# A linear-attention and two-layer feed-forward kernel on one core: the first eight attention units reordered, four weight tiles loaded earlier

## The chip, the cores and the metric

One core of a Trainium2 chip runs the whole program. The metric is the device time in microseconds (us), as the median of several runs.

## The reference, cut to what matters

```python
for t in range(S):                                  # B=4, H=8, S=768, D=64
    state = gamma * state + k[:, :, t] (outer) v[:, :, t]
    y[:, :, t] = scale * q[:, :, t] @ state         # attention with decay
x = y as (3072 tokens, 512)
h = x @ w_in;  x = (h - tanh(h)) @ w_out            # 512 -> 2048 -> 512
h = x @ w_in2; solu = h * softmax(h)                # 512 -> 1024
out = layernorm(solu) * g_ln @ w_out2               # 1024 -> 512
```

The weights arrive as 64-bit floats; the kernel takes them as pairs of 32-bit words and builds single precision from them itself ("decoding").

## The kernel before, in words

The attention is cut into 24 units, numbered k = 4c + b: chunk c of 128 time steps (six) of batch b (four). The linear recurrence becomes, for a unit, a set of small TensorE products of 64x64: **scores** (q against k, and k against v, 64 recorded matmuls and as many weight loads) and **output** (q against the running state, and the masked scores against v: 48 matmuls in chunk 0, 64 in later chunks). Between them the scores are masked into `pr`, and the states `sb` and `sa` are updated.

A unit needs, in this order: two transfers of 512 KB (`z`, the halves with q and k and with k and v), and for each chunk a table `tab` of 256 KB; `prepare(k)` (line 235), which scales q by the table on POOL (L245) and v on ACT (L252, four heads) and POOL (L256, the rest); the scores on PE (L233), their mask (L327, DVE), `sb` (L333 on ACT in chunk 0, L335 on DVE later) and `sa` (L338, DVE); the output on PE (L233), which ACT copies to `xf` (L299, L302, L303) and DVE completes with an addition (L307); and `split_x` (line 340), which splits `xf` into a high and a low part: ACT casts the high part (L345), DVE or POOL subtracts for the low one (L346).

Units 0 to 3 make the first block of 512 tokens, units 4 to 7 the second. The program's first stage works off units 0 to 7, then PE goes on with the first feed-forward layer: `products_h(s, f)` (line 349, L357) multiplies token block s by weight tile f, 12 matmuls of 512 columns, `less_tanh` applies tanh (L364, ACT) and the subtraction (L365, DVE). In the text H(f, b) stands for tile f on block b. Units 8 to 15 are woven between the following H.

A weight tile goes through four steps of `Decoder.to` (line 175): step 0 loads it (`raw`, 512 KB, L125, SP's queue); step 1 is one ACT instruction (L131); step 2 is four DVE instructions (L138, L139, L142, L145); step 3 is a cast on ACT (L154) and a subtraction on DVE (L155), after which ACT's queue issues the store of the decoded tile (L189, `wfd`, 256 KB).

Who sets the order: a scheduler places instructions on each engine by a modelled timeline, except those that `pin` (line 100) keeps in the order of the program. PE's products of this stage are all pinned. In the first stage `prepare`, `unit` (with `amid`) and the decoding of tiles 0 to 2 are pinned on ACT, DVE and POOL too. Loads are not pinned; the transfers that SP issues leave in the order in which the scheduler put them, and an issue that must wait holds up all behind it. `tab` has two buffers, so the table of chunk 2 waits for the last use of the table of chunk 0 (the L245 of unit 3), that of chunk 3 for the L245 of unit 7.

PE's order in the first stage: scores 0, scores 1, output 0, scores 2, output 1, scores 3, ..., output 5, scores 7, output 6, H(0,0), output 7, H(1,0), then the main loop with H(0,1), H(1,1), H(2,0), H(2,1), H(3,0) and so on. In the loop of the first stage (line 655) each turn calls `unit(k, k + 2)`: output of unit k, its copies, `prepare(k + 3)`, the addition, `split_x(k)`, scores of unit k + 2 and their evacuation, in this order on each engine.

Of the kernel before, what the change touches and what calls it, by code (L numbers as in the profile page):

```python
# [29 lines left out]
AF = mybir.ActivationFunctionType  # L30
ALU = mybir.AluOpType
# [4 lines left out]
B, H, S, D = 4, 8, 768, 64  # L36
# [29 lines left out]
def col(p, h):  # L66

    return h ^ (p & 1)
# [21 lines left out]
def body(ctx: ExitStack, tc, z, w_in, w_out, w_in2, w_out2, g_ln, cst, tab, out):  # L90
    nc = tc.nc
# [8 lines left out]
    def pin(ins, on=True):  # L100

        if on:
            tc.keep_in_program_order(ins)

    def t4(shape, dtype, name):
        return big.tile(shape, dtype, tag="t4", name=name)
# [52 lines left out]
    late = [False]  # L159

    def fix(ins):
        pin(ins, late[0])
# [42 lines left out]
    zq, zv, tb, vs, qs, pt, sa, sb, xt = {}, {}, {}, {}, {}, {}, {}, {}, {}  # L205
    xf_of = {}
# [2 lines left out]

    def load_tab(c):  # L210
        tb[c] = stp.tile([P, NP * P], F32, tag="tab", name="tab", bufs=2)
        (nc.sync if c else nc.scalar).dma_start(out=tb[c], in_=tab[c])

    def load_half(k, half):
        t = t4([P, 2, NP, P], F32, "z")
        nc.sync.dma_start(out=t.rearrange("p a b c -> p (a b c)"), in_=z[2 * k + half])
        (zv if half else zq)[k] = t

    def load_units(upto):
        while loaded[0] < min(upto, NU):  # L220
            k = loaded[0]
            if k // B not in tb:
                load_tab(k // B)
            for half in range(2):
                load_half(k, half)
            loaded[0] += 1

    def rows(h):
        return slice(h * D, (h + 1) * D)

    def products(todo):
        for o, a, b in todo:
            pin(nc.tensor.matmul(o, a, b, start=True, stop=True, skip_group_check=True), held[0])  # L233
# [28 lines left out]
    def unit(ko, ks, hold=False, pool=ps_r, tag="r", opool=ps_r, engs=None, amid=None):  # L262

        if ko is not None:
            c, b = divmod(ko, B)
            q, v, po, st = qs.pop(ko), vs.pop(ko), pt.pop(ko), (sa.pop(ko, None), sb.pop(ko))
            w = [opool.tile([P, 2, 4 * D], F32, tag="r", name="out") for _ in range(2)]  # L270
            fr = [t[:, 0, :].rearrange("q (i t) -> q i t", i=2) for t in w]
            y = [t[:, 1, :].rearrange("q (h i t) -> q h i t", h=2, i=2) for t in w]

            steps = range(2) if c else (1,)
            products([
                (
                    fr[h][rows(col(2 * i + odd, h)), i, rows(ab)],
                    st[ab][rows(h), 2 * i + odd, :], q[rows(h), 2 * i + odd, rows(ab)],
                )
                for i in range(2) for ab in steps for odd in range(2) for h in range(2)  # L280
            ])
            products([
                (
                    y[ab][rows(col(p, h)), h, p // 2, :], v[rows(ab), 2 * p + h, :],
                    po[rows(ab), h, p, :],
                )
                for p in range(NP) for ab in range(2) for h in range(2)
            ])
            if hold:
                if b == 0:  # L290
                    xf_of[c] = xfp.tile([P, 2, 2, SB], F32, tag=f"xf{c % 2}", name="xf")
                xf = xf_of[c][:, :, :, b * P : (b + 1) * P]
            else:
                xf = t2([P, 2, 2, P], F32, "xf")
            xa = xf.rearrange("q h i t -> q (h i) t")
            ya = [t.rearrange("q h i t -> q (h i) t") for t in y]
            if c:
                for h in range(2):
                    pin(nc.scalar.copy(xf[:, h, :, :], fr[h]), amid or late[0])  # L299
            else:  # L300
                for h in range(2):
                    pin(nc.scalar.copy(xf[:, h, :, rows(1)], fr[h][:, :, rows(1)]), amid or late[0])  # L302
                pin(nc.scalar.copy(xa[:, :, rows(0)], ya[0]), amid or late[0])  # L303
            if amid:
                amid()
            for ab in steps:
                pin(nc.vector.tensor_tensor(  # L307
                    xa[:, :, rows(ab)], xa[:, :, rows(ab)], ya[ab], ALU.add
                ), amid or late[0])
            if not hold:  # L310
                split_x(c, b, xf, engs or (nc.gpsimd, nc.gpsimd), amid or late[0])
        if ks is not None:
            c = ks // B
            kt, kv, v, q = zq.pop(ks)[:, 1, :, :], zv.pop(ks), vs[ks], qs[ks]
            w = [pool.tile([P, 2, 4 * D], F32, tag=tag, name="sc") for _ in range(2)]
            sc, gn = ([t[:, n, :].rearrange("q (p t) -> q p t", p=NP) for t in w] for n in range(2))
            products([
                (sc[h][rows(ab), p, :], kt[rows(h), p, rows(ab)], q[rows(h), p, rows(ab)])
                for p in range(NP) for h in range(2) for ab in range(2)
            ])  # L320
            products([
                (gn[ab][rows(h), p, :], kv[rows(ab), 0, p, rows(h)], v[rows(ab), 2 * p + h, :])
                for p in range(NP) for ab in range(2) for h in range(2)
            ])
            pr = t2([P, 2, NP, D], F32, "pr")
            for h in range(2):
                pin(nc.vector.tensor_tensor(  # L327
                    pr[:, h, :, :], sc[h], mask.unsqueeze(1).to_broadcast([P, NP, D]), ALU.mult
                ), amid or late[0])
            pt[ks] = pr  # L330
            sb[ks] = stp.tile([P, NP, D], F32, tag="sb", name="sb", bufs=3)
            if c == 0:
                nc.scalar.copy(sb[ks], gn[0])  # L333
            else:
                fix(nc.vector.tensor_tensor(sb[ks], sa[ks], gn[0], ALU.add))  # L335
            if c < NC - 1:
                sa[ks + B] = stp.tile([P, NP, D], F32, tag="sa", name="sa")
                fix(nc.vector.tensor_tensor(sa[ks + B], sb[ks], gn[1], ALU.add))  # L338

    def split_x(c, b, xf, engs, fixed=False):  # L340
        if b == 0:
            xt[c] = [[t4([P, 2, SB], F32R, f"x{n}") for _ in range(2)] for n in "hl"]
        for h in range(2):
            xh, xl = (xt[c][n][h][:, :, b * P : (b + 1) * P] for n in range(2))
            pin(nc.scalar.copy(xh, xf[:, h, :, :]), fixed)  # L345
            pin(engs[h].tensor_tensor(xl, xf[:, h, :, :], xh.bitcast(F32), ALU.subtract), fixed)  # L346
# [14 lines left out]

    def less_tanh(ph, g):
        th = t2([P, SB], F32, "th")
        nc.scalar.activation(th, ph, AF.Tanh)  # L364
        nc.vector.tensor_tensor(g, ph, th, ALU.subtract)  # L365

    def split(g, eng_h, eng_l):
        gh, gl_ = t2([P, SB], F32R, "gh"), t2([P, SB], F32R, "gl")
# [17 lines left out]
    def keep_y(s, py, both=True):  # L386
# [10 lines left out]
    dec1 = Decoder(  # L397
        [w_in[f] for f in range(NF1)] + [w_out[f] for f in range(NF1)], [None] * 2 * NF1, nc.vector,
        True,
    )  # L400
# [222 lines left out]
    spare = dict(pool=ps_y, tag="y")  # L623
# [7 lines left out]
    def step_h(n, b):  # L631
        if b == 0:
            g2[n] = t4([P, 2, SB], F32, "g")
        less_tanh(products_h(b, n, ps_y, "y"), g2[n][:, b, :])

    load_half(0, 0)
    load_tab(0)
    nc.scalar.dma_start(out=con, in_=cst)
    load_half(0, 1)
    loaded[0] = 1  # L640
    load_units(2)
    dec1.to(0, 2)
    load_units(2 * B)
    for k in range(2):
        prepare(k, H // 2, True)
        unit(None, k, **spare)
    for st in (1, 2):
        dec1.to(st, 1, True)
    prepare(2, H // 2, True)

    def ahead(k):
        if k < 2 * B:
            prepare(k, H // 2, True)

    for k in range(2 * B):
        both = (nc.vector, nc.gpsimd) if k < 2 * B - 1 else (nc.vector, nc.vector)
        unit(
            k, k + 2 if k + 2 < 2 * B else None, engs=both,
            amid=lambda: ahead(k + 3), **spare
        )  # L660

        if k == 0:
            for st, n in ((3, 1), (1, 2), (2, 2)):
                dec1.to(st, n, True)
        elif k == 1:
            dec1.to(3, 2, True)
        elif k >= 2 * B - 2:
            if k == 2 * B - 1:
                dec1.to(0, 4)
                for st in (1, 2, 3):  # L670
                    dec1.to(st, 3, True)
            step_h(k - (2 * B - 2), 0)
    gs = {}

    def split_g(n):
# [3 lines left out]
    for n in range(NF1):  # L679
# [8 lines left out]
        k = 2 * B + n - LATER  # L688
# [637 lines left out]
```

## Time and profile before

| what | value |
|---|---|
| median of 3 runs | 842.78 us (841.42 to 842.84) |
| the profiled execution's own time | 840.54 us |
| its span | 838.7 us |
| mean granted TensorE clock over the span | 0.994 |
| PE busy | 813.5 us (97%) |
| DVE, ACT, POOL busy | 547.4, 471.9, 294.5 us |

The span is what the profile records; the profiled execution's own time is 1.8 us above it, and 2.2 us below the median of the three runs. PE's busy time counts overlapping, pipelined matmuls, so a share of 97% says that PE was seldom without a matmul, not that it worked at its peak. Matmuls and weight loads are two kinds of instruction of one queue, recorded as PE and PEld.

### The profile page before, as it was taken

What the parts mean: (1) busy time and instruction counts of PE and PEld (TensorE: products, weight loads), DVE (VectorE), ACT (ScalarE), POOL (GpSimd) and SP (SyncE); (2) the same over time, 40 slices, a digit from 0 to 9 for tenths busy, and PEclk for the clock granted to TensorE, in tenths of its full rate; (3) what the DMA queues carried; (4) which work ended last, traced back from release to release, by engine and by line L of the source; (5) the groups of instructions that cost most, each with busy time, mean ns of one, the idle gap of its engine ahead of it and who ended that gap; (6) DMA issues with size and microseconds to landing.
All of it is one profiled execution on the core that took longest, in us unless ns stands there. A gap on an engine that the chain in (4) does not pass through costs nothing. (4 is left out here: it accounts for less than half of the span.)

```text
span 838.7 us, 16423 instructions
## 1 busy us (share of the span) xinstructions
PE 813.5 (97%) x6296; PEld 670.2 (80%) x6296; DVE 547.4 (65%) x1004; ACT 471.9 (56%) x880; POOL 294.5 (35%) x296
## 2 busy tenths in 40 slices
PE   5699999999999999999999999999999999999998
PEld 4678888788887778888788888888788888888876
DVE  3788984999837687522682988374566566566571
ACT  4646753555446665544571527244677677677662
POOL 4511200081424542443300260162655555455310
PEclk9899999999999999999999999999999999999999
DMA  9667853452878963696593828380977777776693
GB/s 358 241 227 287 302 187 132 137 189 74 310 244 312 359 236 131 241 413 219 198 369 93 293 57 312 101 272 1 202 150 151 151 151 150 151 151 125 126 193 84
DMA packets 168606, 169.43 MB, mean 202 GB/s; under 512 B 105680, under 2 KB 118224, under 8 KB 168528
## 3 DMA queue, kind: packets, MB, share of 16 engines
q1 hardware_dynamic: 160176, 153.51, 61.1%
q10 hardware_dynamic: 8352, 14.87, 5.2%
q8 instruction: 49, 0.80, 0.4%
q14 instruction: 29, 0.24, 0.1%
HBM read 107.02 MB, written 61.34 MB: 201 GB/s over the span
## 5 line engine op out<-in xcount | busy, mean ns | idle before, releaser
L382 PE MATMUL py<-gp,w 128*128 128x512 f32 x768 | 175.6, 389 | 1.5 <-DVE gp L166 1.1
L382 PEld LDWEIGHTS py<-gp,w 128*128 128x128 f32 x768 | 144.1, 188 | 32.1 <-DVE gp L166 1.5
L1062 PE MATMUL po<-w,uh 128*128 128x512 f32 x384 | 106.7, 389 | 0.2 <-ACT uh L1046 0.2
L788 POOL TENSOR_TENSOR hs<-hs,th 128x512 f32<-128x512 f32 x48 | 62.6, 1306 | 118.1 <-ACT th L786 110.8
L1062 PEld LDWEIGHTS po<-w,uh 128*128 128x128 f32 x384 | 72.0, 188 | 15.6 <-ACT uh L1046 0.6
L357 PE MATMUL ph<-xh,w 128*128 128x512 f32 x256 | 82.2, 395 | 0.9 <-DVE w L155 0.9
L382 PE MATMUL py<-gh,w 128*128 128x512 f32 x256 | 79.3, 390 | 0.3 <-ACT gh L370 0.3
L154 ACT CAST w<-wf 128x512 fp32r<-128x512 f32 x70 | 43.0, 619 | 54.6 <-DVE wf L145 47.1
L166 DVE TENSOR_TENSOR gp<-g,gp 128x512 fp32r<-128x512 f32 x64 | 49.3, 780 | 25.9 <-ACT gp L165 25.8
L1062 PE MATMUL po<-w,ul 128*128 128x512 f32 x192 | 63.0, 389 | 0.0
L786 ACT ACTIVATE th<-hs 128x512 f32<-128x512 f32 x48 | 30.4, 632 | 54.0 <-DVE hs L796 52.4
L977 PE MATMUL ph<-w,yhs 128*128 128x512 f32 x192 | 59.2, 390 | 0.7 <-ACT part L984 0.7
L155 DVE TENSOR_TENSOR w<-wf,w 128x512 fp32r<-128x512 f32 x70 | 51.8, 745 | 10.2 <-ACT w L154 9.5
L357 PEld LDWEIGHTS ph<-xh,w 128*128 128x128 f32 x256 | 48.0, 188 | 11.8 <-DVE w L155 1.4
L382 PEld LDWEIGHTS py<-gh,w 128*128 128x128 f32 x256 | 48.0, 188 | 10.7 <-ACT gh L370 0.7
L770 PE MATMUL ph<-xh,wch 128*128 128x512 f32 x140 | 56.4, 403 | 0.0
L770 PE MATMUL ph<-xl,wch 128*128 128x512 f32 x140 | 54.7, 391 | 0.0
L165 ACT CAST gp<-g 128x512 fp32r<-128x512 f32 x64 | 38.8, 617 | 28.3 <-DMA g<-gd 15.5
L770 PE MATMUL ph<-xh,wcl 128*128 128x512 f32 x140 | 54.7, 391 | 0.0
L770 PE MATMUL ph<-xh,wc 128*128 128x512 f32 x168 | 52.7, 390 | 0.3 <-DVE hs L796 0.3
L796 DVE TENSOR_TENSOR hs<-ph,part 128x512 f32<-128x512 f32 x48 | 32.8, 687 | 30.0 <-PE ph L770 17.4
L1050 DVE TENSOR_TENSOR ul<-hn,uh 128x1024 fp32r<-128x1024 f32 x24 | 31.8, 1324 | 31.3 <-ACT uh L1046 31.3
(128 smaller groups left out, 1755.2 us busy)
## 6 DMA issues: line engine op xcount, KB each, us to landing
z<-z SPq DMA_DIRECT2D x48, 512.0 KB, 7.0
g<-gd SPq DMA_DIRECT2D x64, 256.0 KB, 5.2
raw<-w_in SPq DMA_DIRECT2D x24, 512.0 KB, 6.5
raw<-w_out SPq DMA_DIRECT2D x24, 512.0 KB, 4.3
gd<-hs SPq DMA_DIRECT2D x48, 256.0 KB, 4.3
ud<-ut SPq DMA_DIRECT2D x24, 512.0 KB, 3.4
hn<-ud SPq DMA_DIRECT2D x24, 512.0 KB, 7.1
y1d<-ysb SPq DMA_DIRECT2D x24, 256.0 KB, 3.5
```

Source lines behind the costliest of these rows:

```text
L154: pin(nc.scalar.copy(hi, wf), fixed)
L155: pin(eng.tensor_tensor(lo, wf, hi.bitcast(F32), ALU.subtract), fixed)
L165: fix(nc.scalar.copy(h, src))
L166: fix(eng.tensor_tensor(o, src, h.bitcast(F32), ALU.subtract))
L357: nc.tensor.matmul(ph, a[:, k, :], x, start=n == 0, stop=n == 3 * NK - 1), s < 2
L382: nc.tensor.matmul(py[e], a[:, cols], x, start=f == 0 and n == 0, stop=f == NF1 - 1 and n == 2)
L770: nc.tensor.matmul(ph, a, x, start=first and n == 0, stop=n == 5, skip_group_check=True)
L788: fix(eng.tensor_tensor(g, h, th, ALU.subtract))
L796: fix(nc.vector.tensor_tensor(h, ph, part, ALU.add))
L977: nc.tensor.matmul(ph, x[:, r, :], w, start=first and n == 0, stop=n == 5, skip_group_check=True)
L1050: fix(nc.vector.tensor_tensor(ul, uc.pop(i), uh.bitcast(F32), ALU.subtract))
L1062: nc.tensor.matmul(po, a[:, f, :], dec2.w[f][lo], start=n == 0, stop=n == len(todo) - 1)
```

## The change

The first stage is written anew. Loads: the first two weight tiles' loads are moved between the four halves of units 0 and 1 (order: z of unit 0 first half, tile 0, z of unit 0 second half, tile 1, then the z of units 1 to 7), and two more tiles (2 and 3) are loaded right behind the z of unit 7; before, tiles 0 and 1 were behind units 0 and 1, and tiles 2 and 3 were loaded at the end of the stage. The tables of chunk 2 and later are now pinned on SP's queue. Decoding: tile 0 is decoded around unit 0, tile 1 around units 0 and 1 (before: around units 2 and 3); tile 2 still after unit 7. Units: a turn of the loop is now `split_x(k - 2)`, `prepare(k + 1)`, scores of unit k with their evacuation, output of unit k - 1 with its copies and addition. For this `split_x` is called by itself and takes `xf` from a table. While `late[0]` is set, which it now is in the first stage, the L333 copy, `sa` and `sb`, and the tanh and subtraction of H are pinned as well. The low part of unit 7's second half goes to POOL (before: DVE).

```diff
     def load_tab(c):
-        (nc.sync if c else nc.scalar).dma_start(out=tb[c], in_=tab[c])
+        pin((nc.sync if c else nc.scalar).dma_start(out=tb[c], in_=tab[c]), c > 1)
...
-            if amid:
-                amid()
...
-                split_x(c, b, xf, engs or (nc.gpsimd, nc.gpsimd), amid or late[0])
+                xf_of[c, b] = xf
...
-                nc.scalar.copy(sb[ks], gn[0])
+                fix(nc.scalar.copy(sb[ks], gn[0]))
...
-        nc.scalar.activation(th, ph, AF.Tanh)
-        nc.vector.tensor_tensor(g, ph, th, ALU.subtract)
+        fix(nc.scalar.activation(th, ph, AF.Tanh))
+        fix(nc.vector.tensor_tensor(g, ph, th, ALU.subtract))
...
+    late[0] = True
     load_half(0, 0)
     load_tab(0)
     nc.scalar.dma_start(out=con, in_=cst)
+    dec1.to(0, 1)
     load_half(0, 1)
     loaded[0] = 1
-    load_units(2)
     dec1.to(0, 2)
     load_units(2 * B)
-    for k in range(2):
-        prepare(k, H // 2, True)
-        unit(None, k, **spare)
-    for st in (1, 2):
-        dec1.to(st, 1, True)
-    prepare(2, H // 2, True)
...
-    for k in range(2 * B):
-        both = (nc.vector, nc.gpsimd) if k < 2 * B - 1 else (nc.vector, nc.vector)
-        unit(
-            k, k + 2 if k + 2 < 2 * B else None, engs=both,
-            amid=lambda: ahead(k + 3), **spare
-        )
...
-            if k == 2 * B - 1:
-                dec1.to(0, 4)
-                for st in (1, 2, 3):
-                    dec1.to(st, 3, True)
-            step_h(k - (2 * B - 2), 0)
+    dec1.to(0, 4)
+
+    dec1.to(1, 1, True)
+    prepare(0, H // 2, True)
+    dec1.to(2, 1, True)
+    unit(None, 0, **spare)
+    dec1.to(3, 1, True)
+    dec1.to(1, 2, True)
+    prepare(1, H // 2, True)
+    dec1.to(2, 2, True)
+
+    for k in range(1, 2 * B + 2):
+        if 1 < k <= 2 * B:
+            split_x(k - 2, (nc.vector, nc.gpsimd), True)
+        if k < 2 * B - 1:
+            prepare(k + 1, H // 2, True)
         if k < 2 * B:
-            prepare(k, H // 2, True)
+            unit(None, k, amid=True, **spare)
+        elif k == 2 * B:
+            step_h(0, 0)
+        if k <= 2 * B:
+            unit(k - 1, None, amid=True)
+        if k == 1:
             dec1.to(3, 2, True)
+    split_x(2 * B - 1, (nc.vector, nc.gpsimd), True)
+    step_h(1, 0)
+    for st in (1, 2, 3):
+        dec1.to(st, 3, True)
+    late[0] = False
```

## Rows read from the trace of the kernel before

**Rows 1.** The page: PE's busy time, and PE in 40 slices of 21 us.

```profile
PE 813.5 (97%) x6296; PEld 670.2 (80%) x6296; DVE 547.4 (65%) x1004; ACT 471.9 (56%) x880; POOL 294.5 (35%) x296
...
PE   5699999999999999999999999999999999999998
```

**Rows 2.** Windows: columns first, then the first 60 us and 100 to 838 us.

```profile
core 0: us, PE busy (x) PEld busy (x) DVE busy (x) ACT busy (x) POOL busy (x), PEclk, DMA share, GB/s
0.00:60.00 60.00, 42.04 (x1034) 36.76 (x1034) 38.25 (x79) 30.96 (x92) 23.78 (x30) 0.91 0.75 283
...
100.00:838.00 738.00, 731.82 (x4559) 600.71 (x4557) 473.39 (x853) 415.04 (x711) 263.80 (x261) 1.00 0.65 191
```

**Rows 3.** Timeline of PE, 22 to 61 us: start, length, engine; idle before and releaser.

```profile
22.48 0.38 PE L233 MATMUL sc<-vq,z 64*64 64x64 f32 x3 [2.57 <-issue]
...
28.22 0.38 PE L233 MATMUL out<-vq,sb 64*64 64x64 f32 x9 [2.06 <-ACT sb L333]
28.75 0.28 PE L233 MATMUL out<-vq,sb 64*64 64x64 f32 x4
...
32.48 0.43 PE L233 MATMUL out<-vq,sb 64*64 64x64 f32 x8
...
36.15 0.27 PE L233 MATMUL out<-vq,sa 64*64 64x64 f32 x1 [1.10 <-issue]
...
40.23 0.27 PE L233 MATMUL out<-vq,sa 64*64 64x64 f32 x2 [1.95 <-issue]
...
41.07 0.50 PE L357 MATMUL ph<-xh,w 128*128 128x512 f32 x1
...
60.41 0.73 PE L357 MATMUL ph<-xh,w 128*128 128x512 f32 x2 [0.94 <-DVE w L155]
```

**Rows 4.** Windows cut where PE paused or entered a new stretch of code.

```profile
9.98:16.79 6.81, 4.29 (x139) 4.02 (x133) 4.97 (x8) 2.92 (x12) 1.87 (x2) 0.92 1.02 405
16.79:20.50 3.71, 3.12 (x131) 3.01 (x130) 1.38 (x5) 2.28 (x10) 2.42 (x3) 0.69 1.04 411
20.50:28.60 8.10, 4.06 (x127) 3.79 (x126) 5.82 (x12) 4.54 (x15) 3.69 (x5) 0.79 1.01 393
28.60:32.48 3.88, 3.54 (x127) 3.24 (x127) 3.25 (x9) 3.85 (x17) 3.14 (x4) 0.59 0.26 96
32.48:36.00 3.52, 2.44 (x130) 2.16 (x126) 2.85 (x8) 2.33 (x10) 3.45 (x5) 0.97 0.02 5
36.00:40.00 4.00, 2.13 (x126) 1.99 (x127) 3.09 (x10) 2.02 (x6) 1.33 (x3) 1.00 0.74 259
```

**Rows 5.** The page, DMA queues: packets, MB, share of 16 engines.

```profile
q8 instruction: 49, 0.80, 0.4%
```

**Rows 6.** DMA view of 5 to 29.7 us.

```profile
DMA packets 3229, 9.82 MB, mean 397 GB/s; under 512 B 615, under 2 KB 615, under 8 KB 3226
```

**Rows 7.** Waits of SP's queue to 60 us: total, times, longest.

```profile
SPq L212 <- POOL vq L245: 10.4, 1, 10.4
```

**Rows 8.** Timeline of SP's queue, 36 to 54 us.

```profile
36.10 3.24 SPq L125 DMA_DIRECT2D raw<-w_in  x5
41.18 12.66 SPq L216 DMA_DIRECT2D z<-z  x4
```

**Rows 9.** Timeline of POOL: q of units 1 and 7 scaled.

```profile
7.93 1.27 POOL L245 TENSOR_TENSOR vq<-z,tab 128x512 f32<-128x512 f32 x1 [0.27 <-DMA z<-z]
...
34.43 1.27 POOL L245 TENSOR_TENSOR vq<-z,tab 128x512 f32<-128x512 f32 x1
```

**Rows 10.** Timeline of ACT and DVE, 47 to 53 us: tile 2's decoding, tanh.

```profile
47.38 0.67 ACT L131 ACTIVATE wf<-raw 128x512 f32<-128x512 f32 x1
48.18 0.60 ACT L364 ACTIVATE th<-ph 128x512 f32<-128x512 f32 x1
...
52.10 0.69 DVE L155 TENSOR_TENSOR w<-wf,w 128x512 fp32r<-128x512 f32 x1
```

More of the change, by code (lines that the diff above doesn't have):

```diff
@@ L338, in unit, with split_x @@
                 fix(nc.vector.tensor_tensor(sa[ks + B], sb[ks], gn[1], ALU.add))
-    def split_x(c, b, xf, engs, fixed=False):
+    def split_x(k, engs, fixed=False):
+        c, b = divmod(k, B)
+        xf = xf_of.pop((c, b))
         if b == 0:
@@ L638, in body @@
     nc.scalar.dma_start(out=con, in_=cst)
+    dec1.to(0, 1)
     load_half(0, 1)
     loaded[0] = 1
-    load_units(2)
     dec1.to(0, 2)
     load_units(2 * B)
-    for k in range(2):
-        prepare(k, H // 2, True)
-        unit(None, k, **spare)
-    for st in (1, 2):
-        dec1.to(st, 1, True)
-    prepare(2, H // 2, True)
-    def ahead(k):
-        if k < 2 * B:
-            prepare(k, H // 2, True)
-    for k in range(2 * B):
-        both = (nc.vector, nc.gpsimd) if k < 2 * B - 1 else (nc.vector, nc.vector)
-        unit(
-            k, k + 2 if k + 2 < 2 * B else None, engs=both,
-            amid=lambda: ahead(k + 3), **spare
-        )
[L662 to L665, printed above, removed]
-            dec1.to(3, 2, True)
-        elif k >= 2 * B - 2:
-            if k == 2 * B - 1:
-                dec1.to(0, 4)
-                for st in (1, 2, 3):
-                    dec1.to(st, 3, True)
-            step_h(k - (2 * B - 2), 0)
+    dec1.to(0, 4)
[12 more added lines that the diff above has]
+            prepare(k + 1, H // 2, True)
+        if k < 2 * B:
+            unit(None, k, amid=True, **spare)
[4 more added lines that the diff above has]
+        if k == 1:
+            dec1.to(3, 2, True)
+    split_x(2 * B - 1, (nc.vector, nc.gpsimd), True)
[3 more added lines that the diff above has]
+    late[0] = False
     gs = {}
```

## The prediction

> **What bounds the kernel now.** I read the page first: PE is busy in 97% of the span, and its slices stand at 9 in all but the first two and the last [rows 1]. Then the windows: of 738 us after the first 100, PE is idle for 6.2 (738.00 - 731.82), but of the first 60 us for 18.0 (60.00 - 42.04) [rows 2]. So the time is a first stage of about 41 us, until H(0,0) starts at 41.07 [rows 3], and behind it a PE that hardly stops. PE's order behind that point is not changed, so what moves the start of H(0,0), which I call T0, moves the end by as much. The change acts on the first stage alone.
>
> Next, what ended PE's pauses in that stage. The reader is to see in the timeline that the three late ones have no releaser: 2.57 us before 22.48, 1.10 before 36.15 and 1.95 before 40.23 are put down to "issue", that is, PE's queue had nothing to wait for and still did not go on [rows 3]. Now the count: between the pauses lie 253 recorded instructions (126 + 127), then 254 and 256, then 253 [rows 4]; the two windows before these are cut by counting back, and hold 272 and 261, since instructions that lie across a cut count twice. And the instruction queue moved 49 packets for 2 x 6296 recorded matmuls and weight loads, 257 to a packet, 0.80 MB in all [rows 1, 5]. So PE stops where a new block of 256 instructions begins, and what it lacks is its own code: entering a block frees room for the next, whose fetch then has to arrive before that is entered. The entries are at 9.98, 16.79, 22.48, 28.75, 32.48, 36.15 and 40.23 [rows 3, 4]; I call them blocks 1 to 7. H(0,0) follows 0.84 us into block 7.
>
> The distances between entries are the point. Where the transfers fill the queues (DMA share 1.0) they are 5.69 and 6.27 us; with the queues empty (share 0.02 to 0.26) 3.73 and 3.67; with five tiles starting to load 4.08 [rows 3, 4]. In the fourth distance lies a wait of 2.06 us for the L333 copy [rows 3], but its end at 28.22 comes before the entry at 28.75. So from 16.79 on, I read the first stage as a chain of five fetches, 23.4 us long (40.23 - 16.79), that no other engine sets: over the last four windows of rows 4, 19.5 us, DVE is busy 15.0, ACT 12.7 and POOL 11.6 [rows 4]. That the queues were empty from 30 to 36 us is an accident of SP's order: the table of chunk 3 held the queue for 10.4 us until POOL had scaled the q of unit 7 (34.43 + 1.27 = 35.70) [rows 7, 9], and the five weight tiles left at 36.10 [rows 8].
>
> The Trainium skill ("Runtime: NRT & Kernel Launch", section "Instruction fetch mechanics") has the same blocks of 256 instructions, but says that crossing a boundary is "mostly hidden". The trace agrees with the first and not, in this stage, with the second; what the second would give is a rival below.
>
> **The change, part by part.** PE's products are the same, and walking through the new loop gives the same order: scores 0, scores 1, output 0, scores 2, and so on to scores 7, output 6, H(0,0), output 7, H(1,0). So the block boundaries stay where they are, and a gain can come only from earlier entries or faster fetches.
>
> *Tiles 0 and 1 ahead of unit 1.* Two loads of 512 KB move ahead of the z of unit 1. At 397 GB/s [rows 6] that is 2.6 us. POOL scales unit 1's q as soon as z lands: it ended at 9.20, and block 1 was entered 0.78 later [rows 4, 9]. So block 1 is now entered at about 12.6. Units 2 to 7 have the same bytes ahead of them as before. Block 2 was entered 6.81 us after block 1, waiting for unit 2's data; that data comes no later, but the fetch started 2.6 later, and with full queues it needs 5.7 (block 3's distance, the shortest seen under load): 18.3, or +1.5.
>
> *Blocks 3 and 4* are fetched under full queues as before: 24.0 and 29.7 at 5.7 each (22.48 and 28.75 before).
>
> *Tiles 2 and 3 behind unit 7, and the tables pinned.* The two tiles add 2.6 us of full queues behind 29.7. More weighs what follows: with the tables kept behind tiles 4 to 6, nothing stops SP's queue any more, and tiles 4, 5, 6 and the z of units 8 and 9, which left from 36.10 to about 44 [rows 8], follow at once: three tiles 3.9 us, a table 0.7, three halves of z 3.9, to about 40.8. So the empty stretch that made blocks 5 and 6 quick (3.73 and 3.67) is filled. At 5.7 each, block 5 is entered at 35.4 and block 6 at 41.1. Block 7 then has empty queues: 3.7, so 44.8. T0 is 0.84 later, 45.6, against 41.07: **+4.6 us**. The bounds of these fetches: 5.7 to 6.3 (with full queues) and 3.7 to 4.1 (block 7); with the larger ones T0 is 48.9 (+7.9). With 3.7 from block 5 on it is 41.6 (+0.5).
>
> *The reordering of units.* Evacuation of scores, scaling, copies and splits keep their number and sizes, and only their order on ACT, DVE and POOL changes; one unit's split no longer stands between its output and the next unit's scaling. I cost this at nothing. It removes the 2.06 us wait for L333, which the fetch of block 4 hides. What hides the rest is again the fetch: a block leaves each engine 5.7 us and the busiest stretch above asks 5.82 of DVE in 8.10 [rows 4]. If that cover is gone, it is worth what the first rival says.
>
> *Tile decoding earlier.* The same eight DVE and four ACT instructions, now in the first 20 us, where DVE was busy 1.38 of 3.71 us before block 3 [rows 4]. Nothing on PE waits for w before H(0,0). Nothing either way.
>
> *After T0.* Tanh of H(1,0) is now ahead of tile 2's first step on ACT. Before, that step ran at 47.38 and the tanh at 48.18 [rows 10]; behind the tanh the step starts at about 48.8, 1.4 later. Tile 2's low part ended at 52.79 (52.10 + 0.69), and H(2,0), the fifth H of 2.7 us from 41.07 with one output between, needs it at about 53.7. So 0.9 of the 1.4 is slack and up to 0.5 is lost; DVE in turn loses one subtraction (the low part on POOL), about 0.4. The 0.94 us that H(3,0) waited for its tile [rows 3] may go or stay, since DVE and not the load set it. I take zero, with -0.9 and +0.5 as ends. A half clock when H starts is possible, as the clock share in rows 4 falls to 0.59 where PE paused much: 2.7 us of H would take twice as long, so up to +2.7; before it was 1.00 from 36 on, and I take zero.
>
> **Sum.** 840.54 us of the profiled execution + 4.6 = 845.1. That execution lies 2.2 below the median of the runs shown, so against the median 842.8 + 4.6 = **847.4 us**, slower.
>
> **The rivals.**
> 1. *The data bounds the stage, and the change frees it: faster.* If PE's pauses at the boundaries were only waits that the trace fails to name, or the fetches ran far ahead once engines wait less for each other, T0 would be set by the last z: it lands at 29.7 as before, scaling takes 1.3, two blocks of PE work at 2.1 to 3.5 busy [rows 4] at most another 4: T0 about 34, -7: 835.8 us. It decides if block 3 to block 7 follow at under 3.5 us. The skill's "mostly hidden" speaks for it. For it too: the L333 wait, and output 6 waiting behind long chains on ACT and DVE. Against it: three nameless pauses, each at a multiple of 256. Chance 0.10.
> 2. *The queues run empty after tile 3.* The tables may still hold SP's queue, or the loads of tiles 4 to 6 may wait for buffers. Then block 5 takes something between (4.7), blocks 6 and 7 3.7 each: 34.4, 38.1, 41.8, T0 42.6: +1.5, 844.3. For it: in the trace before, just this happened [rows 7]. Against it: the pinning of the tables. Chance 0.22, half of it within 0.2%.
> 3. *No difference.* Fetches as quick as any seen (3.7 from block 5 on), T0 41.6, and the wait of H(3,0) gone: -0.4, 842.4. Chance 0.12.
> 4. *Slower still*: fetches of 6.3, or the half clock: about 850.7. Chance 0.06.
>
> My forecast of +4.6 has 0.50.
>
> **How the numbers follow.** A difference under 0.2% (1.7 us) is about what the measurement cannot tell from none. Faster: rival 1 and a little for unforeseen gains behind T0, since the scheduler places all later unpinned work anew: 0.12. Same: rival 3 and half of rival 2, less a little, 0.20. Slower: the forecast, half of rival 2 and rival 4, 0.68. The range leaves out rival 1 below and the end of rival 4 above: 841.5 to 850.5.
>
> **What would show it.** Right: H(0,0) starts between 44 and 47 us; the pauses marked "issue" grow and still lie 256 instructions apart; block 1 entered at about 12.6; SP's queue without a long wait for POOL, the five tiles leaving before 30 us, and full queues to about 40. Wrong: H(0,0) before 39, or PE's pauses in the stage ended by DMA, ACT or DVE by name; then the fetch is not what binds. Empty queues from 33 us on speak for rival 2. If T0 is late but the end is not, the stage behind it had slack that I do not see.

## The result, and the profile after

The changed kernel took 848.94 us (median of 6 runs, 848.43 to 850.47), the kernel before 840.92 in the same job (6 runs, 840.15 to 842.84). The ratio is 1.0093, 95% interval 1.0075 to 1.0112: **slower by 8.0 us**. I had forecast slower by 4.6 us, and 847.4; the direction and the range held, more than a third of the loss was not in my sum, and most of the loss that did come had another cause than the one I gave. All ratios in this document go by fast runs alone, which leaves out one execution of run e7 (1650.95 us).

The page of the kernel after, in the parts of [rows 1] and [rows 5]: busy times, PE in 40 slices, the instruction queue.

```profile
PE 810.1 (96%) x6296; PEld 666.9 (79%) x6296; DVE 544.8 (64%) x1003; ACT 471.9 (56%) x880; POOL 293.6 (35%) x297
...
PE   1589999999999999999999999999999999999997
...
q8 instruction: 49, 0.80, 0.4%
```

The span is 847.3 us (before 838.7). The number of PE's instructions and the packets of its code are the same as before; in the slices the first two differ most, the first with a tenth of its time busy instead of half. The windows of the kernel after, with the columns of [rows 2]:

```profile
0.00:60.00 60.00, 30.36 (x999) 26.57 (x1000) 27.60 (x64) 25.97 (x82) 22.74 (x30) 1.00 0.63 244
...
15.00:23.00 8.00, 0.00 (x0) 0.00 (x0) 0.00 (x0) 0.00 (x0) 0.00 (x0) 1.00 1.03 408
...
100.00:838.00 738.00, 734.79 (x4692) 603.52 (x4691) 483.30 (x873) 421.70 (x735) 265.43 (x263) 1.00 0.66 194
```

The middle line is the finding: for 8 us none of the five engines did anything at all, while the transfers ran at 408 GB/s. Behind the first 100 us PE is as full as before.

Where it is lost is seen in the timeline of PE in the kernel after (start, length; idle before and releaser), beside [rows 3]:

```profile
11.70 1.14 PE L233 MATMUL sc<-vq,z 64*64 64x64 f32 x32 [1.80 <-POOL vq L245]
...
25.31 1.52 PE L233 MATMUL sc<-vq,z 64*64 64x64 f32 x29 [12.47 <-ACT vq L252]
...
34.12 0.28 PE L233 MATMUL sc<-vq,z 64*64 64x64 f32 x3 [0.56 <-issue]
...
38.16 0.28 PE L233 MATMUL out<-vq,sb 64*64 64x64 f32 x4 [1.70 <-issue]
...
41.63 0.21 PE L233 MATMUL out<-vq,sa 64*64 64x64 f32 x1 [1.09 <-issue]
...
45.26 0.27 PE L233 MATMUL out<-vq,sa 64*64 64x64 f32 x1 [0.54 <-issue]
...
48.97 0.27 PE L233 MATMUL out<-vq,sa 64*64 64x64 f32 x2 [0.54 <-issue]
49.81 0.50 PE L357 MATMUL ph<-xh,w 128*128 128x512 f32 x1
```

One pause of 12.47 us stands in the middle of scores 1: the low half of unit 1's v, which ACT scales, is not there. H(0,0) starts at 49.81, 8.74 later than before, and from there to the end of the span it is 797.5 us (847.3 - 49.8) against 797.6 before. So the whole loss is made ahead of H(0,0), as I had argued; the pause makes it. What held ACT is in the timeline of ACT in the kernel after:

```profile
10.65 0.62 ACT L154 CAST w<-wf 128x512 fp32r<-128x512 f32 x1
23.98 0.34 ACTq L189 DMA_DIRECT2D wfd<-wf  x1
24.36 0.66 ACT L131 ACTIVATE wf<-raw 128x512 f32<-128x512 f32 x1 [13.09 <-DMA z<-z]
24.93 2.00 ACT L252 ACTIVATE vq<-z,con 128x64 f32<-128x64 f32 x8
```

Tile 0's cast ends at 11.27. The next thing in ACT's queue is the issue of the store of that tile (L189), and it goes only at 23.98. The profile puts the wait on the instruction behind it, tile 1's first step (13.09 us, "DMA z<-z"), because the profile keeps an issue as a row of the queue (ACTq) and not as an operation of the engine. Tile 1 itself had landed long before; the z that came last is the second half of unit 5, which landed at 23.96 and has nothing to do with either. The order of ACT's instructions in the compiled program explains the name:

```
9 L154 CAST w<-wf 128x512
10 L189 DMA wfd_71<-wf 128x512 [waits DMAHW0_49]
11 L131 ACTIVATE wf<-raw 128x512 [waits DMAHW5_49]
12 L252 ACTIVATE vq<-z,con 128x64 [waits DMAHW7_49]
```

The compiled program has eight completion counters (DMAHW0 to DMAHW7), which all transfers of SP and ACT use in turn, and it makes a transfer that is to use a counter wait until the one that used it before has landed. The store's counter, DMAHW0, was last given to the second half of unit 5's z, and with queues as full as in [rows 6] that lands late. Behind the store on ACT stand tile 1's first step and then the scaling of v of units 1 and 2, which need none of it. In the kernel before, the same wait is there and nearly harmless: tile 0's store is issued when most of the z are in, and the L131 behind it waited 1.8 us for "DMA z<-z". The timeline of ACT in the kernel before:

```profile
22.73 0.33 ACTq L189 DMA_DIRECT2D wfd<-wf  x1
23.11 0.67 ACT L131 ACTIVATE wf<-raw 128x512 f32<-128x512 f32 x1 [1.80 <-DMA z<-z]
```

### The profile page after: what moved, and what is told of

It is laid out like the page before. It is cut to its first block, busy times and chain, and to the rows that moved or that the text cites. A ratio compares the mean times of both kernels' runs of the same rounds, so it can differ in the third digit from the quotient of the medians.

```text
span 847.3 us, 16429 instructions
## 1 busy us (share of the span) xinstructions
PE 810.1 (96%) x6296; PEld 666.9 (79%) x6296; DVE 544.8 (64%) x1003; ACT 471.9 (56%) x880; POOL 293.6 (35%) x297
## 5 line engine op out<-in xcount | busy, mean ns | idle before, releaser
L166 DVE TENSOR_TENSOR gp<-g,gp 128x512 fp32r<-128x512 f32 x64 | 49.9, 789 | 26.5 <-ACT gp L165 26.4
```

What stands on the lines that cost most here:

```text
L166: fix(eng.tensor_tensor(o, src, h.bitcast(F32), ALU.subtract))
```

## The experiments

In each timeline of this section the first columns are start and length, and brackets hold the idle time before and what ended it. Ratios are to the kernel before, run in the same job (its medians 841.56, 841.62 and 841.74 us). By "entries" I mean the entries of blocks 1 to 7 of PE's code, as in the prediction.

### The stores of the first two tiles

**Run e1_after_stores_late**: the kernel after, the stores of tiles 0 and 1 collected and issued on ACT behind H(1,0).

```diff
-                        pin(nc.scalar.dma_start(out=to, in_=wf), fixed)
+                        if self.put_off is None:
+                            pin(nc.scalar.dma_start(out=to, in_=wf), fixed)
+                        else:
+                            self.put_off.append((to, wf))
...
     step_h(1, 0)
+    dec1.store()
```

> The changed kernel with the stores of the decoded tiles 0 and 1 issued behind unit 7 instead of right behind their decoding. Store theory: ACT's issue of the first store waits for the landing of the z transfer whose semaphore it reuses (23.96 us), and all of ACT behind it. Then PE's pause from 12.84 to 25.31 us is gone, block 2 is entered at about 18, H(0,0) starts between 42 and 46 instead of at 49.81, and the time is 841 to 845 us. Load theory (the loss comes from unit 1's later z and from fetches under full queues alone): the pause only changes its name, H(0,0) stays at 49 to 50, and the time at 848 to 849.

845.89 us, 1.0047 (1.0029 to 1.0064), a little above the 845 that I expected. PE's timeline:

```profile
11.89 2.03 PE L242 MATMUL sc<-vq,z 64*64 64x64 f32 x64 [1.83 <-POOL vq L254]
...
18.16 0.80 PE L242 MATMUL sc<-vq,z 64*64 64x64 f32 x18 [1.69 <-issue]
...
24.24 0.38 PE L242 MATMUL sc<-vq,z 64*64 64x64 f32 x3 [1.06 <-issue]
...
30.52 0.28 PE L242 MATMUL out<-vq,sb 64*64 64x64 f32 x4 [2.71 <-issue]
...
44.19 0.69 PE L366 MATMUL ph<-xh,w 128*128 128x512 f32 x1
```

The pause of 12.47 us is gone, scores 1 run in one piece, and the entries are 18.16, 24.24 and 30.52 where the prediction had 18.3, 24.0 and 29.7. H(0,0) starts at 44.19 instead of 49.81. Of these 5.6 us only 3.3 reach the end of the span (847.3 - 844.0): from H(0,0) on it holds 799.8 us (844.0 - 44.2), 2.3 more than after. The timeline of SP's queue shows the z of unit 8 leaving at 54.23, behind a wait of SP for a store ("SPq L225 <- DMA wfd<-wf", 21.9 us the longest): the late stores hold the shared counters at a new place.

**Run e8_after_stores_mid**: the same, the stores issued after turn k = 5 of the loop.

```diff
+        if k == 5:
+            dec1.store()
```

> The changed kernel with the stores of tiles 0 and 1 issued behind output 4, where the transfers whose semaphores they reuse have landed. Store theory: as in the run with late stores, block 2 at about 18, H(0,0) at 43.5 to 45, and since the stores no longer hold up the z of unit 8 the 2 us that were lost behind H(0,0) come back: 842.5 to 845. If those 2 us have another cause: 845 to 846.5.

844.07 us, 1.0021 (1.0008 to 1.0035); entries 18.41, 24.67, 30.94, 36.98, 40.34, 44.20, H(0,0) at 45.05, and 797.8 us behind it (842.8 - 45.05), as before. PE's timeline:

```profile
18.42 0.59 PE L242 MATMUL sc<-vq,z 64*64 64x64 f32 x18 [2.44 <-issue]
...
45.05 0.50 PE L366 MATMUL ph<-xh,w 128*128 128x512 f32 x1
```

The z of unit 8 leaves from 41.26 on, and the loss behind H(0,0) is gone, which is what I held against e1's late stores. This is the cleanest test: apart from the two stores, the compiled programs have the same instructions in the same order on PE, DVE, ACT and POOL as the kernel after. So **the place of the two stores alone is worth more than half of the 8 us**: 4.5 us by the spans of the profiled executions (847.3 - 842.8), some 6 us by the ratios (0.93% - 0.21% = 0.72%, each with an interval of 0.13 to 0.19 points to either side). The H(0,0) that results, 45.05, is close to the 45.6 of the prediction. Of the 4.0 us by which it is later than before, the ratio shows about 1.8 us at the end; part of that gap is that the profiled execution of the kernel before (840.54 us) was one of its quick ones.

**Run e13_after_stores_on_sp**: the kernel after, all stores on SP's queue instead of ACT's.

```diff
-                        pin(nc.scalar.dma_start(out=to, in_=wf), fixed)
+                        nc.sync.dma_start(out=to, in_=wf)
```

> The changed kernel with one edit: the stores of decoded tiles are issued by SP, so ACT never waits for a transfer's semaphore. Store theory: PE's pause of 12.5 us is gone, block 2 is entered at about 18, H(0,0) starts at 42 to 45.5; SP is held behind the store of tile 2, so the queues run empty after tile 3 and blocks 5 to 7 follow at 3.5 to 4.5 us. Time 3 to 6 us below the changed kernel. Load theory: the pause stays under another name, 848 to 849 us.

853.25 us, 1.0139 (1.0122 to 1.0155). In the first stage the order on PE, DVE, ACT and POOL is that of the kernel after: the pause is gone, entries 12.43, 17.99, 24.33, 30.33, 34.17, 37.93 and 41.88, and H(0,0) at 42.72, 7.1 earlier than after. Not all of the 7.1 is the pause: SP issues no load between 25.28 and 53.84, so the queues run empty, and blocks 5 to 7 follow at 3.8 to 4.0 us. The total missed what I expected, because SP now stands behind the stores. The timelines of its queue and of PE:

```profile
25.28 28.46 SPq L189 DMA_DIRECT2D wfd<-wf  x2
53.84 0.88 SPq L125 DMA_DIRECT2D raw<-w_in  x2
...
62.96 1.83 SPq L216 DMA_DIRECT2D z<-z  x4
```

```profile
69.02 1.13 PE L233 MATMUL sc<-qs,z 64*64 64x64 f32 x32 [2.93 <-POOL qs L245]
```

The store of tile 2 waits for its decoding (26.9 us), SP with it, and the z of unit 8 leaves at 62.96 instead of 34 to 41; PE waits for its scaling. The group of SP's waits to 200 us (total, times, longest):

```profile
SPq L189 <- DVE wf L145: 120.1, 19, 26.9
```

**Run e12_before_stores_on_sp**, the control: the same edit in the kernel before.

```diff
-                        pin(nc.scalar.dma_start(out=to, in_=wf), fixed)
+                        nc.sync.dma_start(out=to, in_=wf)
```

> The kernel before with the stores issued by SP. The control for the two others: H(0,0) at 40.5 to 41.5 (fetch), time within 1.5 us of before.

855.66 us, 1.0177 (1.0154 to 1.0199): in the time a miss. H(0,0) starts at 41.55, 0.5 from before, so the stage gains nothing there; the rest lost 12 us to SP's waits (107.8 us, 19 times, behind DVE L145). Moving a queue's issue to another queue moves the wait, with all that stands behind it.

### Loads, tables and PE's code

**Run e2_before_tables_pinned**: the kernel before with the pinned tables alone, so that SP's queue is not held in front of tiles 2 to 6.

```diff
-        (nc.sync if c else nc.scalar).dma_start(out=tb[c], in_=tab[c])
+        pin((nc.sync if c else nc.scalar).dma_start(out=tb[c], in_=tab[c]), c > 1)
```

> The kernel before with one edit, the tables of chunk 2 and later pinned, so that tiles 2 to 6 no longer wait behind the table of chunk 3. The order on PE, DVE, ACT and POOL is the same as before. Fetch theory: the queues are full where they were empty (30 to 36 us), the entries of blocks 5 and 6 come 4.5 to 6 us apart instead of 3.7, H(0,0) starts at 42.5 to 45.5 instead of 41.07, and the time is 1.5 to 4.5 us above before. Rival (the pauses named issue do not hang on the transfers): H(0,0) within 0.5 us of 41.07, the time within 1 us of before.

843.50 us, 1.0025 (1.0015 to 1.0034). Windows cut at the entries of blocks 4 to 7 (columns of [rows 2]):

```profile
28.50:34.70 6.20, 3.68 (x126) 3.50 (x127) 4.80 (x13) 3.88 (x15) 5.40 (x6) 0.50 1.03 406
34.70:39.60 4.90, 3.69 (x127) 3.50 (x126) 2.27 (x7) 2.23 (x8) 1.43 (x3) 0.50 0.81 303
39.60:43.10 3.50, 3.39 (x125) 3.40 (x127) 1.01 (x4) 1.10 (x4) 0.00 (x0) 0.50 0.02 5
```

The five tiles leave from 24.14 instead of 36.10 [rows 8], and the stretch that had been empty is full. Each of these windows holds 253 or 252 recorded instructions. The first takes 6.20 us at a DMA share of 1.03 and the second 4.90 at 0.81; in the kernel before they took 3.73 and 3.67. The third takes 3.50 at 0.02, but there PE is busy for 3.39 us at the lower clock level, so that block is PE's own work and no wait. H(0,0) moved from 41.07 to 44.29. The order on all engines is that of the kernel before, so this run shows that the transfers beside them lengthen PE's blocks here.

The packets of PE's code (the instruction queue, 16 KB each) stand in the traces with their times, and they show which part grows. In this run the packet started 3.7 us after the entry at 28.50, 2.8 us after that at 34.73, and 1.1 us after that at 39.71. In the kernel before it started 3.1 to 3.8 us after the entries of blocks 1 to 3, and 1.1 us after those of blocks 4 and 5, under empty queues. The packet itself took 0.9 to 1.2 us, and PE entered the next block 1.3 to 1.6 us after its end wherever it stood waiting for code. So what grows under the transfers is the time until the packet starts.

**Run e4_before_new_loads**: the kernel before with the new order of all loads and the pinned tables; units and decoding as they were.

```diff
+    dec1.to(0, 1)
     load_half(0, 1)
...
-    load_units(2)
     dec1.to(0, 2)
     load_units(2 * B)
+    dec1.to(0, 4)
```

> The kernel before with the change's order of loads alone (tile 0 and 1 between the halves of unit 0 and ahead of unit 1, tiles 2 and 3 behind unit 7, tables pinned); units and decoding in the old order. Store theory: tile 0 is decoded as late as before, so its store finds its semaphore free or nearly so, no pause over 3 us, H(0,0) at 42.5 to 46, time 1.5 to 5 us above before. Load theory: the loads carry nearly the whole loss, H(0,0) at 48 to 50, time 7 to 9 us above before.

844.39 us, 1.0034 (1.0023 to 1.0045). PE's timeline:

```profile
18.42 0.51 PE L233 MATMUL sc<-vq,z 64*64 64x64 f32 x18 [1.56 <-issue]
...
24.61 0.38 PE L233 MATMUL sc<-vq,z 64*64 64x64 f32 x3 [3.31 <-issue]
...
30.89 0.38 PE L233 MATMUL out<-vq,sb 64*64 64x64 f32 x4 [0.82 <-issue]
...
36.02 0.26 PE L233 MATMUL out<-vq,sa 64*64 64x64 f32 x1 [1.45 <-issue]
...
41.27 0.27 PE L233 MATMUL out<-vq,sa 64*64 64x64 f32 x1 [1.56 <-issue]
...
45.07 0.27 PE L233 MATMUL out<-vq,sa 64*64 64x64 f32 x2 [1.67 <-issue]
45.92 0.50 PE L357 MATMUL ph<-xh,w 128*128 128x512 f32 x1
```

One pause, of 3.31 us, is longer than the 3 us that I expected; it is one of the code's. This is the chain of the prediction, entry by entry: 12.82, 18.42, 24.61, 30.89, 36.02, 41.27, 45.07 and H(0,0) at 45.92, where it had 12.6, 18.3, 24.0, 29.7, 35.4, 41.1, 44.8 and 45.6. So the terms that I wrote for loads and tables were right up to H(0,0), and right about a kernel that has only these edits. Of the 4.8 us at H(0,0), 3.7 remain in the span (842.4 against 838.7) and 2.8 in the medians: with tiles 2 and 3 there early, H(3,0) no longer waits for its tile [rows 3].

### The order of the units

**Run e9_new_unit_order_only**: the kernel before with the new loop and the added pins; loads, tables and decoding stay as near to before as the loop lets them, and the stores of tiles 0 and 1 are issued after turn k = 5, to keep their wait out.

```diff
+    prepare(0, H // 2, True)
+    unit(None, 0, **spare)
+    prepare(1, H // 2, True)
+    for k in range(1, 2 * B + 2):
+        if 1 < k <= 2 * B:
+            split_x(k - 2, (nc.vector, nc.gpsimd), True)
+        if k < 2 * B - 1:
+            prepare(k + 1, H // 2, True)
+        if k < 2 * B:
+            unit(None, k, amid=True, **spare)
...
+        if k <= 2 * B:
+            unit(k - 1, None, amid=True)
...
+        if k == 5:
+            dec1.store()
```

> The change's order of units alone: loads in the order of before, tables not pinned, tiles 0 and 1 decoded around units 1 to 3 as before, their stores behind output 4. Fetch theory: the order on ACT, DVE and POOL is worth nothing, since the entries of blocks 3 to 7 are set by the fetch: H(0,0) at 40.5 to 41.8, time within 1 us of before. Rival (the held pipeline is worth something by itself): H(0,0) before 39, time over 2 us below before.

844.90 us, 1.0037 (1.0024 to 1.0050): a miss. I had costed the order at nothing. PE's timeline, then POOL's:

```profile
21.36 2.08 PE L242 MATMUL sc<-vq,z 64*64 64x64 f32 x64 [2.40 <-POOL vq L254]
...
28.31 2.09 PE L242 MATMUL sc<-vq,z 64*64 64x64 f32 x64 [3.35 <-POOL vq L254]
...
34.34 2.05 PE L242 MATMUL sc<-vq,z 64*64 64x64 f32 x63 [2.44 <-POOL vq L254]
```

```profile
25.73 0.85 POOL L355 TENSOR_TENSOR xl<-xf,xh 128x256 fp32r<-128x256 f32 x1 [3.40 <-ACT xh L354]
26.54 1.71 POOL L254 TENSOR_TENSOR vq<-z,tab 128x512 f32<-128x512 f32 x1
```

In the new order POOL's part of `split_x(k - 2)` stands ahead of the scaling of unit k + 1. It waits for a cast that ACT does at the end of a chain (output, copies, addition), 3.40 us in the row, and the scaling, whose z is long there, stands behind it. 26.54 + 1.71 is 28.25, and PE goes on at 28.31. So the order, with its pins and the small shifts of decoding and stores that the loop brings, costs 0.37% here.

**Run e10_new_order_scale_first**: e9 with `prepare(k + 1)` ahead of `split_x(k - 2)`.

```diff
-        if 1 < k <= 2 * B:
-            split_x(k - 2, (nc.vector, nc.gpsimd), True)
         if k < 2 * B - 1:
             prepare(k + 1, H // 2, True)
+        if 1 < k <= 2 * B:
+            split_x(k - 2, (nc.vector, nc.gpsimd), True)
```

> The run with the new order of units alone, with one swap: in a turn, the scaling of unit k + 1 ahead of the split of unit k - 2. POOL theory: PE's four waits for POOL's vq (2.40, 3.35, 2.44 and 1.53 us) came from POOL's low part of unit k - 2 standing ahead of the scaling in POOL's queue; swapped, they shrink to under 1 us each, H(0,0) starts at 41 to 42.5 instead of 44.52, time 1.5 to 3.5 us below that run, about that of before. Rival (the half clock or the decoding between the units made that run slow): H(0,0) at 43.5 or later, the time within 1 us of that run.

843.69 us, 1.0027 (1.0015 to 1.0038). H(0,0) starts at 42.43 instead of 44.52, as expected; the three POOL waits of the rows above are gone, and a new one takes part of their place in PE's timeline:

```profile
30.26 0.71 PE L242 MATMUL out<-vq,sb 64*64 64x64 f32 x16 [3.32 <-ACT sb L340]
```

The medians differ by 1.2 us, below the 1.5 to 3.5 that I expected, and the two intervals overlap, so a gain in the total is not shown. The run confirms the mechanism on POOL; it does not make the order free.

In the kernel after, this price is mostly covered. There POOL's scaling holds PE for 2.48 us once, at 32.41, and twice for 0.65 (43.10 and 46.81), but these pauses lie inside blocks whose successor is still being fetched. The loads alone (e4, +0.34%) and the order alone (e9, +0.37%) do not add up to both with earlier decoding (e8, +0.21%). What the order costs within the kernel after I can't give more closely.

### Attempts to gain

**Run e5_before_h_between**: the kernel before, H(0,0) and H(1,0) between earlier units, to fill the pauses.

```diff
+        elif k in (4, 5):
+            step_h(k - 4, 0)
...
-            step_h(k - (2 * B - 2), 0)
```

> The kernel before with H(0,0) and H(1,0) (24 instructions and 2.7 us each) moved from behind output 6 and output 7 to behind scores 6 and scores 7. Fetch theory: PE multiplies while the code of blocks 6 and 7 arrives, so most of the pauses of 1.10 and 1.95 us is filled, and the time is 1.5 to 3 us below before. Rival (PE's pauses are only shifted, because every later unit waits as long again): within 0.7 us of before.

844.28 us, 1.0031 (1.0018 to 1.0044): a miss. H(0,0) starts at 35.05, but PE then pauses at a later place, for 2.63 us without a releaser and 2.08 us for ACT. PE's timeline:

```profile
48.15 0.34 PE L233 MATMUL out<-pr,vq 64*64 64x64 f32 x6 [2.63 <-issue]
...
50.56 0.80 PE L357 MATMUL ph<-xh,w 128*128 128x512 f32 x1 [2.08 <-ACT xh L345]
...
54.17 1.05 PE L357 MATMUL ph<-xh,w 128*128 128x512 f32 x2
...
56.13 0.62 PE L357 MATMUL ph<-xh,w 128*128 128x512 f32 x2
```

The granted clock is 0.50 from 48.61 to 55.44, the 1.2 GHz level; PE had paused for 2.63 us shortly before it fell. The matmuls of H show the price: a pair takes 1.05 us there and 0.62 behind it.

**Run e6_before_tiles_held**: the kernel before, the loads of tiles 2 to 6 kept behind a small marker store in the turn of unit 6, so that the queues stay empty under blocks 5 to 7.

```diff
+                pin(nc.sync.dma_start(out=mark, in_=xf[0:1, 0, 0, 0:D]))
+                held_raw[0] = True
+                dec1.to(0, 4)
+                held_raw[0] = False
```

> The kernel before, with the loads of tiles 2 to 6 held on SP until unit 6's xf is complete (a 256 B store of one xf row to a scratch tensor stands ahead of them). Fetch theory: the queues are empty while the code of blocks 6 and 7 is fetched, so block 7 is entered 3.5 to 3.8 us after block 6 (4.08 before) and H(0,0) starts 0.3 to 0.5 us earlier; nothing else is late, since tile 2 is not decoded before about 47. Time 0 to 0.8 us below before. Rival (the fetch does not mind the transfers): the same distance, the time within 0.5 us either way.

841.45 us, 0.9998 (0.9987 to 1.0009). Block 7 was entered 4.35 us after block 6 (35.68 to 40.03), no sooner than before (4.08), though the tiles were held: the packet of PE's code moved at 37.33, while a table was still loading. So the tiles were not what lengthened this block. The table was the only other transfer in that stretch; whether it lengthened the block was not tested.

**Run e7_tiles_held_h_split**: e6, with the first H in two halves of six matmul groups around the turn k = 5.

```diff
+        if k == 5:
+            step_h(0, 0, turn_of_unit)
+        else:
+            turn_of_unit()
```

> The kernel of the run with held tiles, with H(0,0) cut in halves of six matmuls, one ahead of output 5 and one behind scores 7. Fetch theory: the halves (1.4 us each) fill the pauses of blocks 6 and 7, the entries stay where they are within 0.5 us, H(1,0) starts at 42 to 43 instead of 45.12, and the time is 2 to 3 us below before. Rival (the pauses are only shifted): H(1,0) at 44.5 to 45.5, the time within 1 us of before.

841.24 us, 0.9998 (0.9989 to 1.0008). The halves fill the pauses (entries 32.74, 36.58, 40.32, 43.84) and H(1,0) starts at 42.23 instead of 45.12, but the gain is given back at once. PE's timeline:

```profile
57.61 0.50 PE L366 MATMUL ph<-xh,w 128*128 128x512 f32 x1 [0.66 <-ACT w L154]
...
59.10 0.73 PE L366 MATMUL ph<-xh,w 128*128 128x512 f32 x2 [0.75 <-DVE w L155]
```

PE waits for the decoding of the next tiles and then for v of unit 8, and output 8 starts at 72.40 in both kernels. The H that start earlier meet weights and units that don't come earlier.

**Run e11_h_split_stores_on_sp**: e7, stores on SP's queue.

```diff
-                        pin(nc.scalar.dma_start(out=to, in_=wf), fixed)
+                        nc.sync.dma_start(out=to, in_=wf)
```

> The run with tiles held and H(0,0) in halves, with the stores of decoded tiles issued by SP instead of ACT. If what gave the gain back there were ACT's issues of stores that wait for a semaphore (64.02 us, ahead of unit 8's scaling), unit 8's scores come at 64 with no long wait behind them and the time is 1.5 to 3 us below before. If it is DVE's decoding, or SP is now held by the stores and the z of unit 8 comes late: within 1 us of before, or above.

852.60 us, 1.0127 (1.0104 to 1.0149), by the same waits of SP as in e12 and e13 (102.1 us behind DVE L145). No version that I tried is faster than the kernel before.

## Why the prediction was right or wrong

- *The end moves with H(0,0).* Right for this change: H(0,0) +8.74, span +8.6. As a rule it was too strong: e7 moved H(1,0) forward by 2.9 us for nothing, and in e4 part of a loss was made up.
- *Tiles 0 and 1 ahead of unit 1.* Right: block 1 is entered at 12.43, predicted 12.6.
- *Tile decoding earlier: "Nothing either way".* **This is the step that failed.** I counted eight DVE and four ACT instructions and asked who waits for w. I left out that each decoded tile also issues a store on ACT's queue (L189), what that issue waits for, and what stands behind it on ACT. The store moved from a time when most z had landed to one when they had hardly begun, waited 12.7 us (11.27 to 23.98), and unit 1's v stood behind it. Block 2 was entered at 28.71 instead of 18.3: +10.4. e1, e8 and e13 each take the pause away by moving the issue alone.
- *Blocks 3 and 4 under full queues; blocks 5 and 6 too.* Right as a mechanism (e2, e4), wrong for this kernel, because the pause let the loads run ahead. The distances after are 5.41, 4.04, 3.47, 3.62 and 3.72, 20.3 us in all where I had 26.5: -6.2. Windows of the kernel after, cut near the entries:

```profile
28.71:34.10 5.39, 2.37 (x141) 2.09 (x133) 3.45 (x8) 4.88 (x18) 3.88 (x5) 1.00 1.04 409
34.10:38.14 4.04, 2.34 (x127) 2.14 (x126) 3.04 (x9) 2.66 (x10) 2.71 (x4) 1.00 0.96 336
38.14:41.60 3.46, 2.38 (x126) 2.14 (x127) 1.59 (x5) 2.01 (x8) 1.82 (x3) 1.00 0.20 78
...
45.20:48.90 3.70, 2.52 (x126) 2.24 (x127) 2.65 (x9) 1.85 (x7) 2.59 (x4) 1.00 0.02 4
```

  From 38 us on the queues are empty and the blocks take 3.5 to 3.7; only the block under a share of 1.04 takes over 5. The packet of code started 2.85 us after the entry at 28.71, and 1.0 to 1.3 us after the later ones, also in the block of 4.04 us with a mean share of 0.96: the share of a whole block is a rough sign. The two errors, +10.4 and -6.2, make the 4.2 us by which H(0,0) is later than the 45.6 of the sum. That the number came near is in good part this cancelling.
- *The tables pinned.* Right as to POOL: tiles 4 to 6 left from 26.62 to 31.4 and not at 36.10, without a long wait for it. Wrong as to "nothing stops SP's queue any more": behind two halves of the z of unit 8 it stood for 27.3 us. Waits of SP's queue to 70 us in the kernel after (total, times, longest):

```profile
SPq L216 <- DMA wfd<-wf: 28.7, 2, 27.3
```

  It is the same kind of wait as ACT's: the next half was to use the counter of a store that ACT had not yet issued. So the queues ran empty at 38 us and were not full to about 40.
- *"The reordering of units: nothing".* Wrong by itself (e9, +0.37%), nearly harmless here because the fetches cover it. I named the cover, but not the instruction that would be late: the scaling behind POOL's half of the split.
- *After H(0,0): zero.* Right: 797.5 us against 797.6, with the 0.94 of H(3,0) gone.
- *The clock.* No cost: the granted clock is 1.00 (2.4 GHz) in every window of the kernel after that is shown. e2's first stage ran at 0.50 (1.2 GHz) from 23.3 to 43.8, and still its two long blocks ended in pauses of 2.54 and 1.28 us; in e5, e11 and e13 (there from 68.56 to 75.39) the lower level met the matmuls of H.
- *The rivals.* Rival 1 (the data bounds, 835.8 us) falls by e2 and e4: in e2 the z of units 0 to 7 are loaded as before, and its blocks grew, with pauses of 2.5 and 1.3 us that carry no releaser. The Trainium skill ("Runtime: NRT & Kernel Launch", section "Instruction fetch mechanics") calls the crossing of a block "mostly hidden"; these runs disagree for this stage, with pauses of 0.8 to 3.3 us at the crossings in e4. Rival 2 (queues empty behind tile 3) is in its result what blocks 5 to 7 did, but for another reason, the counter that held SP. None of the rivals held a wait of an issue on ACT.

What I had said would prove me wrong, "PE's pauses in the stage ended by DMA, ACT or DVE by name", came: the pause of 12.47 us carries ACT's name. Of what I had said would show it right, the start of H(0,0) between 44 and 47 us did not come (49.81), and the pauses marked "issue" did not grow (0.54 to 1.70 us, before 1.10 to 2.57).

## What to carry to other kernels

When a step moves earlier, list every instruction that it issues, the stores too, and for each issue ask which earlier transfer must land before it may go and what stands behind it on that engine's queue: an issue on a computing engine can stop that engine for as long as the transfers ahead take (12.7 us here). In a stage of many small PE instructions, count them in blocks of 256 and look at the DMA share beside each block before loads are moved into an empty stretch. And test a moved part alone and in its setting, since prices that hide behind one another don't add.

## What the runs showed of the hardware that was not expected

- The issue of a transfer on ACT waited 12.7 us for the landing of an unrelated transfer of SP, by a completion counter that the compiled program gives to both in turn (e1, e8 and e13: gone when the issue is elsewhere). The wait appears in the profile under the next instruction of the engine, with the name of the unrelated transfer.
- All engines idle for 8 us with transfers at 408 GB/s (15 to 23 us of the kernel after): a full DMA share says nothing of whether the data is needed at that moment.
- A block of 256 PE instructions took 6.20 us beside full queues and 4.90 at a share of 0.81 in neighbouring windows of one run (e2), and 3.60 to 3.70 with empty queues in the kernel after. The packet of code started 3.1 to 3.8 us after the entry of a block under full queues (kernel before, blocks 1 to 3) and 1.1 us after it with empty ones (blocks 4 and 5), and took 0.9 to 1.2 us in both cases.
- Stores on SP's queue waited 102 to 120 us in the first 200 us for DVE, and the kernels with that edit are 1.3% to 1.8% slower than the kernel before, although SP does no work of its own.
